# Two linear-attention branches on one core: key-value products by column tiles, a ring of numerator tiles, the Z sums by halves

## The chip, the core and the metric

One of the eight cores of a Trainium2 chip runs the whole program. The metric is the device time of one execution in microseconds; the time given for a kernel is the median of its runs. The core has five engines that run side by side, each through its own list of instructions in order, tied together by semaphores: TensorE (PE in the profile, with its weight loads as PEld), VectorE (DVE), ScalarE (ACT), GpSimd (POOL) and SyncE (SP), which issues DMA transfers. A matmul has a stationary operand (loaded by LDWEIGHTS) and a moving one, and writes to PSUM, which holds eight banks of 512 f32 per partition.

## The reference, cut to what matters

```python
# x: 2048 tokens x 640; 32 heads of 20
def A(x):                                   # branch A
    q, k, v = heads(x @ wqkv)
    phi_q = [softmax(q @ w_phi), softmax(-(q @ w_phi))]      # 40 features a head
    phi_k = the same of k
    kv  = einsum('bhsf,bhsd->bhfd', phi_k, v)
    z   = sum over tokens of phi_k
    num = einsum('bhqf,bhfd->bhqd', phi_q, kv)
    den = einsum('bhqf,bhf->bhq', phi_q, z) + 1e-6
    return (num / den) @ wo
def B(x):                                   # branch B: four segments of 512 tokens
    # causal softmax inside a segment, mixed by sigmoid(beta) with a
    # memory M, z that sums elu features of the earlier segments
    ...
out = g * A(x) + (1 - g) * B(x)             # g = sigmoid(x . gate_w)
```

## The kernel before, in words

The order on all five engines is written out by hand: each engine executes its instructions in the order in which the code emits them. The stages are these.

**Keys and values of branch A** (L300 to L324). After the weights are folded and turned, a loop over 16 chunks of 128 tokens computes keys and values (L235), the two signs of exponentials of the keys (L239, ACT), their sums per head (L243, DVE) and the normalised features `EkSn` (L247, POOL). Each chunk of `EkSn` is also moved by DMA into `Z`, 32 rows of 640 per partition, so that the token sum becomes 31 additions of whole rows (L261, DVE). Then the query weights are folded (L326).

**Key-value products** (L404 to L419). The 640 features are five blocks `j` of 128. For a block and a sign, `emit_kv` (L358) adds 16 matmuls, one a chunk: the stationary operand is 128 features of 128 tokens, the moving one the values of the heads that these features touch (7 heads, 140 columns; 8 heads in two pieces of 80 for block 2). That is 192 matmuls. Only the features of the same head are wanted of each product; `emit_kvn` (L380, DVE) multiplies by a mask and writes `kvn`. The last two chunks of blocks 0, 1, 3, 4 come after the first 14 of all four. On DVE the additions of Z stand among the `emit_kvn`: nine before, four between, 18 after.

**Queries of branch A** (L515 to L527). For two halves of the tokens and five blocks, `emit_pq` computes ten matmuls of 512 columns and ACT takes the exponentials of both signs (L401). All PSUM tiles up to here are of one pool of four tiles of two banks. After the fifth block TensorE turns the finished Z row (`emit_z`, L266). After the sixth, DVE sums 32 sub-rows of it (L274, 31 dependent additions of 20 columns) and writes the denominator weights `kvd` (L277). After the ninth, `emit_den` computes the denominators of chunks 0 to 3, and after the tenth DVE and POOL turn them into scales (`first_chain`, L494).

**The chunk loop of branch A** (L583 to L629). For each of 16 chunks and both signs: TensorE computes the numerators (`emit_num`, L438, six matmuls into one of two PSUM tiles), DVE multiplies them by the scales (`emit_tt`, L487), POOL adds the two signs (L604), and a DMA transposes the sum. TensorE fills its time with 36 halves of projections of branch B (`emit_half`, L546: five matmuls of 320 columns; keys and queries of five chunks, values of eight), whose results ACT copies out. A denominator tile in a bank of its own receives the denominators of the next four chunks (L597); the halves use three more banks. ACT also makes features of keys here (L625 to L627, L618).

**Branch B** (L635 on). 16 steps of two head groups for scores (L679), their exponentials (L683, ACT), triangle masks (L690, POOL), products with values (L735), divisions (`emit_epi`, L755, DVE and POOL), and the remaining projections as filling, by a written plan. Its PSUM pools are, in order, `bst` (two tiles of two banks, scores), `bnd` (`nda`, two banks) and `bps` (two banks). The last part finishes four chunks of rows and writes them out.

Of the kernel before, what the change touches and what calls it, by code (L numbers as in the profile page):

```python
# [15 lines left out]
def kernel(  # L16
# [212 lines left out]
    def emit_a1(sc):  # L229
# [17 lines left out]
        nc.gpsimd.tensor_tensor(  # L247
# [11 lines left out]
    def emit_zadd(ts):  # L259
        for t in ts:  # L260
            nc.vector.tensor_tensor(out=Z[:, 0, :], in0=Z[:, 0, :], in1=Z[:, t, :], op=ALU.add)  # L261
# [7 lines left out]
    def emit_zz(zt_ps):  # L269
        nc.vector.tensor_copy(out=zt, in_=zt_ps)  # L270
        ztv = zt.rearrange("p j (s a h b) -> p j s h b a", s=2, h=2, b=2)
        nc.vector.tensor_copy(out=zz, in_=ztv[:, :, :, :, 0, 0])
        for w in range(1, 32):
            nc.vector.tensor_tensor(out=zz, in0=zz, in1=ztv[:, :, :, :, w // 16, w % 16], op=ALU.add)  # L274
        nc.vector.tensor_tensor(out=zcol, in0=zz[:, :, :, 0], in1=zz[:, :, :, 1], op=ALU.add)
        for sgn in range(2):
            nc.vector.tensor_tensor(out=kvd[:, sgn, :, :, 0], in0=wmask,  # L277
                                    in1=zcol[:, :, sgn:sgn + 1].to_broadcast([P, KC, H]), op=ALU.mult)
# [79 lines left out]
    def emit_kv(j, sgn, scs):  # L358
        h0, h1 = (P * j) // DH, (P * j + P - 1) // DH + 1
        bk, off = int(j > 2), 0  # L360
        n = (h1 - h0) * DH
        b0 = h0 // 16
        if (sgn, j) not in kv_tiles:
            kv_tiles[sgn, j] = w2tile("kv_ps")
            if j < 2:
                kv_tiles[sgn, j + 3] = kv_tiles[sgn, j]
        for sc in scs:
            if h1 <= 16 or h0 >= 16:
                o = 321 * b0 + (h0 - 16 * b0) * DH
                parts = [(off, vA[:, sc].rearrange("p b n -> p (b n)")[:, o:o + n])]  # L370
            else:
                n0 = (16 - h0) * DH
                parts = [(off, vA[:, sc, 0, h0 * DH:320]),
                         (off + n0, vA[:, sc, 1, 0:n - n0])]
            for o, rhs in parts:
                nc.tensor.matmul(kv_tiles[sgn, j][:, bk, o:o + rhs.shape[-1]],
                                 lhsT=EkSn[:, sc, sgn, j * P:(j + 1) * P], rhs=rhs,
                                 start=(sc == 0 and o == off), stop=(sc == NCH - 1 and o == parts[-1][0]))

    def emit_kvn(j, sgn):  # L380
        h0, h1 = (P * j) // DH, (P * j + P - 1) // DH + 1
        g0 = TH[j][0]
        nc.vector.tensor_tensor(
            out=kvn[:, sgn, j, h0 - g0:h1 - g0, :],
            in0=kv_tiles[sgn, j][:, int(j > 2), 0:(h1 - h0) * DH].rearrange("p (h d) -> p h d", d=DH),
            in1=wmw[:, j, h0 - g0:h1 - g0, None].to_broadcast([P, h1 - h0, DH]), op=ALU.mult)
# [4 lines left out]
    def emit_pq(qb, j):  # L391
        Eq = Eq0[:, j] if qb == 0 else a3e.tile([P, 2, HB], BF16, name="Eq")
        pq = w2tile("pq")
        for half in range(2):
            for c in range(KC):
                nc.tensor.matmul(pq[:, half, :], lhsT=WqA[:, c, j * P:(j + 1) * P],  # L396
                                 rhs=xq[:, 2 * qb + half, c],
                                 start=(c == 0), stop=(c == KC - 1))
        pqf = pq.rearrange("p b n -> p (b n)")
# [4 lines left out]
    emit_zadd(range(1, 10))  # L404
    PAIRS = [(js, sgn) for js in ((0, 3), (1, 4)) for sgn in range(2)]
    for js, sgn in PAIRS:
        for j in js:
            emit_kv(j, sgn, range(14))
    for js, sgn in PAIRS:
        for j in js:  # L410
            emit_kv(j, sgn, range(14, NCH))
        for j in js:
            emit_kvn(j, sgn)
    emit_zadd(range(10, 14))
    for sgn in range(2):
        emit_kv(2, sgn, range(NCH))
        emit_kvn(2, sgn)
    emit_gate()
    emit_zadd(range(14, 32))  # L419
# [14 lines left out]

    BATCH = [list(range(c, c + 4)) for c in range(0, NCH, 4)]
    NB = 4

    def emit_num(ch, sgn):  # L438
        qb, qc = divmod(ch, HB // P)
        t = nps.tile([P, 2, 512], F32, name=f"num{sgn}")  # L440
        for n, (j, bk, lo, hi) in enumerate(PIECES):
# [4 lines left out]
                             start=(n in FIRST), stop=(n in LAST))  # L446
        return t[:, :, 0:320].rearrange("p b (h e) -> p b h e", e=DH)

    def emit_den(t, ch, k):
        qb, qc = divmod(ch, HB // P)  # L450
        for sgn in range(2):
            for j in range(KC):
                nc.tensor.matmul(t[:, k, sgn].rearrange("p h e -> p (h e)"),
# [4 lines left out]
    def den_tile():  # L458
        return dps.tile([P, NB, 2, H, 2], F32, name="den")

    def emit_rr(t, n, o=0):
        rr = a3w.tile([P, NB, 2, H], F32, name="rr")
        nc.vector.reciprocal(out=rr[:, 0:n], in_=t[:, o:o + n, :, :, 1])
        return rr, emit_uu(t, rr, n, o)

    def emit_uu(t, rr, n, o):
        uu = a3w.tile([P, NB, 2, H], F32, name="uu", bufs=1)
        nc.vector.tensor_tensor(out=uu[:, 0:n], in0=t[:, o:o + n, :, :, 0], in1=rr[:, 0:n], op=ALU.mult)
        return uu

    def emit_dsum(uu, n):
# [3 lines left out]
        return dd  # L475

# [17 lines left out]
    def first_chain(dt):  # L494
        rr, uu = emit_rr(dt, NB)
# [19 lines left out]
    for qb in range(2):  # L515
        for j in range(KC):
            emit_pq(qb, j)
            if (qb, j) == (0, KC - 1):
                z_den = w2tile("z_den")
                zt_ps = emit_z(z_den[:, 0])  # L520
            if (qb, j) == (1, 0):
                emit_zz(zt_ps)
                open_stages()
            if (qb, j) == (1, 3):
                dt = z_den[:, 1].rearrange("p (k s h e) -> p k s h e", k=NB, s=2, e=2)
                for n in range(NB):
                    emit_den(dt, n, n)  # L527
    emit_gS()
    first_chain(dt)
    aps_stack.close()  # L530
    nps_stack = ExitStack()
    nps, dps, last_pps, pps = [nps_stack.enter_context(tc.tile_pool(
        name=n, bufs=b, space=bass.MemoryType.PSUM, reuse_waits="tile"))
        for n, b in (("nps", 1), ("dps", 1), ("last_pps", 1), ("pps", 2))]
    oTA = resB.tile([P, NCH + 1, KC, P], BF16, name="oTA")
    Msb = resB.tile([P, G, 4, DH + 1], F32, name="Msb")
    Mbd = resB.tile([P, G, 4, DH + 1], BF16, name="Mbd")

    def emit_half_mm(ps, part, sc, half):
        W = {"k": WkB, "q": WqB, "v": WvB}[part]  # L540
        for cc in range(KC):
            nc.tensor.matmul(ps, lhsT=xq[:, sc // 4, cc, sc % 4 * P:(sc % 4 + 1) * P],  # L542
                             rhs=W[:, cc, half * 320:(half + 1) * 320],
                             start=(cc == 0), stop=(cc == KC - 1))

# [18 lines left out]
    for vB in vBs:  # L564
        nc.gpsimd.memset(vB[:, :, :, DH:DH + 1], 1.0)
# [3 lines left out]
              for half in range(2)]  # L569

    def emit_next_half():
        if halves:
            emit_half(last_pps if len(halves) % 3 == 1 else pps, *halves.pop(0),
# [6 lines left out]
    nums = [emit_num(0, 0)]  # L580
    emit_next_half()
    nums.append(emit_num(0, 1))
    for ch in range(NCH):  # L583
# [4 lines left out]
        for sgn in range(2):  # L588
            emit_tt(tt, sgn, nums[sgn], cs_of[ch])
            emit_next_half()  # L590
            if (ch, sgn) in ((4, 1), (9, 1), (14, 1)):
                emit_next_half()
            if ahead and k < 2 and sgn == 0:
                if k == 0:
                    dt = den_tile()
                for n in range(2):
                    emit_den(dt, ahead[2 * k + n], 2 * k + n)  # L597
            if ch + 1 < NCH:
                nums[sgn] = emit_num(ch + 1, sgn)
            if ahead and k == 2 and sgn == 0:  # L600
                uu = emit_uu(dt, rr_n, NB, 0)
# [4 lines left out]
        if ahead and k < 2:  # L606
            if k == 0:
                rr_n = a3w.tile([P, NB, 2, H], F32, name="rr")
            nc.vector.reciprocal(out=rr_n[:, 2 * k:2 * k + 2], in_=dt[:, 2 * k:2 * k + 2, :, :, 1])
# [6 lines left out]
        if ch >= NCH - 2:  # L616
            part = "kq"[ch - NCH + 2]
# [3 lines left out]
        if k == 1:  # L621
            key = stages["k"][(ch // 4) % 2][:, :, 0:DH]
            phik = phiks[0][:, ch // 4, :, 0:DH]
            ek = a3w.tile([P, H, DH], BF16, name="ek")
            nc.scalar.activation(out=ek, in_=key, func=ACT.Relu, scale=-1.0)  # L625
            nc.scalar.activation(out=ek, in_=ek, func=ACT.Exp, scale=-1.0)
            nc.scalar.activation(out=phik, in_=key, func=ACT.Relu)  # L627
        if k == 3:
            nc.gpsimd.tensor_tensor(out=phik, in0=phik, in1=ek, op=ALU.add)  # L629
# [5 lines left out]
    with ExitStack() as bctx:  # L635
# [5 lines left out]
        bst = bctx.enter_context(tc.tile_pool(name="bst", bufs=2, space=bass.MemoryType.PSUM,  # L641
# [3 lines left out]
        bps = bctx.enter_context(tc.tile_pool(name="bps", bufs=2, space=bass.MemoryType.PSUM,  # L645
                                              reuse_waits="tile"))
        oBs, ogs = {}, {}

# [9 lines left out]
        class Step:  # L658
            def __init__(self, k):
                self.s, self.g = divmod(k, G)  # L660
                self.PT = {}
                self.last = k == NSEG * G - 1
                if self.g == 0:
# [63 lines left out]
        def pv_items(st, js):  # L727
            vB = vBs[st.s % 2]

            def piece(j, i):  # L730
                if j == 0 and i == 0 and not st.last:
                    st.nda = bnd.tile([P, 2, 512], F32, name="nda")
# [276 lines left out]
        first_nda = bnd.tile([P, 2, 512], F32, name="nda")  # L1009
        for half in range(2):  # L1010
            banks[1, half] = first_nda[:, half, 0:320]
# [21 lines left out]
        for n, half in ((0, 0), (0, 1), (1, 0), (1, 1)):  # L1033
            turned_mm(n, half, (4,))
# [47 lines left out]
```

## Time and profile before

| | us |
|---|---|
| median of 3 runs (lowest, highest) | 323.62 (323.53, 323.63) |
| the profiled execution, its own time | 324.17 |
| its span, first to last instruction | 322.4 |
| keys, values, folding | 0 to 56.4 |
| key-value products | 56.4 to 66.9 |
| queries, Z, first denominators | 66.9 to 89.9 |
| chunk loop of branch A | 89.9 to 131.8 |
| branch B | 131.8 to 309.5 |
| last rows | 309.5 to 322.4 |

The stages are read off the timeline by the first matmul of each. TensorE is busy for 309.2 us of the span, ScalarE for 252.1, VectorE for 224.7, GpSimd for 208.5. The granted TensorE clock is full in all 40 slices. Busy times of TensorE are modelled: a matmul of 512 columns is shown with 0.38 us, while two such follow each other by 0.216 us, so rates are read from the starts of long rows of matmuls and not from the mean duration.

### The profile page before, as it was taken

How to read it: one execution, taken by the hardware profiler on the slowest of the kernel's cores; microseconds unless marked ns; L12 is line 12 of the kernel's file. 1: busy time of each engine (PE TensorE's matmuls, PEld its weight loads, DVE VectorE, ACT ScalarE, POOL GpSimd, SP SyncE). 2: the span in 40 equal slices, each digit the busy share in tenths (PEclk: the TensorE clock that was granted, in tenths of full speed). 3: DMA queues.
4: the chain of work that ended last, by engine and by line, in shares of the span. 5: the costliest groups of instructions: out<-in, count | busy, mean ns of one | idle time of the engine just before them, and what ended most of it. 6: DMA issues, size and time to landing. Idle time of an engine off the chain costs nothing.

```text
span 322.4 us, 9493 instructions
## 1 busy us (share of the span) xinstructions
PE 309.2 (96%) x3901; PEld 213.5 (66%) x3904; DVE 224.7 (70%) x447; ACT 252.1 (78%) x322; POOL 208.5 (65%) x308
## 2 busy tenths in 40 slices
PE   8999999999999999989999999999999999999995
PEld 7888877964577788555566566656656656655663
DVE  3477997998799797477768577676866745454463
ACT  4777888248945545999998999999998998898953
POOL 8588599302268789756657667677776676666550
PEclk9999999999999999999999999999999999999999
DMA  7948835691016797876231363462476372322132
GB/s 223 218 105 195 204 105 139 190 368 61 0 35 111 113 148 94 160 100 84 52 67 35 66 107 68 87 101 54 79 109 93 72 121 60 76 76 50 47 87 81
DMA packets 91812, 34.19 MB, mean 106 GB/s; under 512 B 79866, under 2 KB 91770, under 8 KB 91770
## 3 DMA queue, kind: packets, MB, share of 16 engines
q1 hardware_dynamic: 91194, 32.95, 50.5%
q10 hardware_dynamic: 576, 0.66, 0.7%
q8 instruction: 30, 0.49, 0.7%
q14 instruction: 12, 0.10, 0.1%
HBM read 6.42 MB, written 2.62 MB: 28 GB/s over the span
## 4 chain that ended last, share of the span: by engine, by line
PE 37%; ACT 22%; DVE 3%; issue 2%; POOL 0%; ACTq 0%; DVEq 0%
ACT PT L683 19%; PE st_ps L679 9%; PE proj L813 7%; PE nda L735 6%; PE proj L869 5%; PE proj L542 3%; PE num L443 2%; DVE td L772 1%; PE nda L748 1%; PE nda L743 1%; DVE rec L762 1%; ACT ek L841 1%; PE nda L991 1%; DVE rec L760 1%; DVE Eq L845 1%
## 5 line engine op out<-in xcount | busy, mean ns | idle before, releaser
L683 ACT ACTIVATE PT<-st_ps 128x1024 bf16<-128x1024 f32 x160 | 153.8, 1024 | 14.7 <-PE st_ps L679 12.5
L690 POOL TENSOR_SCALAR_AFFINE_SELECT PT<-PT 128x512 bf16<-128x512 bf16 (+1 forms) x130 | 85.4, 675 | 48.5 <-ACT PT L683 48.3
L735 PEld LDWEIGHTS <-PT 128*128 128x128 bf16 x1280 | 39.8, 96 | 10.3 <-issue 6.5
L247 POOL TENSOR_TENSOR EkSn<-Ek,krec 128x1280 bf16<-128x1280 bf16 x16 | 37.4, 2360 | 9.1 <-DVE krec L246 8.3
L735 PE MATMUL nda<-vB,PT 128*128 128x21 bf16 x1240 | 41.4, 173 | 0.7 <-DVE mtmp L778 0.6
L869 PEld LDWEIGHTS <-xTf 128*128 128x128 bf16 x300 | 26.5, 97 | 16.0 <-issue 7.1
L875 DVE CAST Z<-proj 128x320 bf16<-128x320 f32 x44 | 20.8, 487 | 22.2 <-PE proj L869 21.8
L235 PEld LDWEIGHTS <-xTf 128*128 128x128 bf16 x240 | 27.1, 113 | 5.9 <-DVE xTf L200 0.3
L243 DVE TENSOR_REDUCE ksum<-Ek 128x64 f32<-128x1280 bf16 x16 | 23.6, 1475 | 8.0 <-ACT Ek L239 8.0
L489 DVE TENSOR_TENSOR tt<-num,rr 128x640 f32<-128x640 f32 x32 | 24.8, 802 | 4.9 <-POOL rr L482 2.2
L239 ACT ACTIVATE Ek<-pk 128x640 bf16<-128x640 f32 x32 | 20.8, 702 | 9.4 <-PE pk L235 8.4
L679 PE MATMUL st_ps<-Z 32*128 32x512 bf16 (+3 forms) x256 | 24.7, 299 | 3.5 <-ACT PT L683 2.9
L604 POOL TENSOR_TENSOR oA<-tt 128x640 bf16<-128x640 f32 x16 | 24.6, 1548 | 4.6 <-DVE tt L489 3.4
L813 PE MATMUL proj<-WkA,oTA 128*128 128x320 bf16 x160 | 27.1, 299 | 0.3 <-DMA oTA<-oA 0.3
L679 PE MATMUL st_ps<-Eq 32*128 32x512 bf16 (+3 forms) x256 | 24.5, 299 | 2.3 <-ACT PT L683 1.8
L775 POOL TENSOR_TENSOR oB<-td 128x320 bf16<-128x320 f32 x22 | 19.5, 886 | 6.5 <-DVE td L772 4.9
L401 ACT ACTIVATE Eq<-pq 128x1024 bf16<-128x1024 f32 x20 | 19.4, 1021 | 5.4 <-PE pq L396 5.4
L813 PE MATMUL proj<-WvA,oT 128*128 128x320 bf16 x120 | 22.2, 300 | 0.5 <-DVE oTA L822 0.5
L396 PE MATMUL pq<-xTf,WqA 128*128 128x512 bf16 x97 | 21.9, 379 | 0.2
L772 DVE TENSOR_TENSOR td<-nda,rec 128x640 f32<-128x640 f32 x23 | 19.0, 825 | 2.1
L542 PEld LDWEIGHTS <-xTf 128*128 128x128 bf16 x180 | 16.3, 97 | 4.4
L443 PE MATMUL num<-kvn,Eq 128*128 128x240 bf16 (+2 forms) x192 | 18.0, 229 | 0.6 <-DVE tt L489 0.6
(174 smaller groups left out, 552.8 us busy)
## 6 DMA issues: line engine op xcount, KB each, us to landing
Z<-EkSn SPq DMA_DIRECT2D x32, 160.0 KB, 2.7
out_dram<-orow SPq DMA_DIRECT2D x8, 160.0 KB, 1.8
out_dram<-oTA SPq DMA_DIRECT2D x6, 160.0 KB, 1.9
WvA<-in_A_wqkv_dram SPq DMA_DIRECT2D x2, 400.0 KB, 6.3
WkB<-in_B_wk_dram SPq DMA_DIRECT2D x1, 800.0 KB
WqB<-in_B_wq_dram SPq DMA_DIRECT2D x1, 800.0 KB, 6.9
WvB<-in_B_wv_dram SPq DMA_DIRECT2D x1, 800.0 KB, 9.6
WkA<-in_A_wo_dram SPq DMA_DIRECT2D x1, 800.0 KB, 11.3
```

Of the source, the lines that this page charges most:

```text
L235: nc.tensor.matmul(ps[:, bk, 0:n], lhsT=key_tokens(c, sc), rhs=rhs, start=(c == 0), stop=(c == KC - 1))
L247: nc.gpsimd.tensor_tensor(out=EkSn[:, sc].rearrange("p s (h f) -> p (s h) f", f=DH), in0=Ek.rearrange("p s (h f) -> p (s h) f", f=DH), in1 ...
L443: nc.tensor.matmul(t[:, bk, (lo - 16 * bk) * DH:(hi - 16 * bk) * DH], lhsT=Eqs[qb, j][:, sgn, qc * P:(qc + 1) * P], rhs=kvn[:, sgn, j, lo ...
L489: nc.vector.tensor_tensor(out=tt[:, sgn].rearrange("p (b h) d -> p b h d", b=2), in0=ps, in1=csb, op=ALU.mult)
L542: nc.tensor.matmul(ps, lhsT=xq[:, sc // 4, cc, sc % 4 * P:(sc % 4 + 1) * P], rhs=W[:, cc, half * 320:(half + 1) * 320], start=(cc == 0), s ...
L604: nc.gpsimd.tensor_tensor(out=oA.rearrange("p (h d) -> p h d", d=DH), in0=tt[:, 0], in1=tt[:, 1], op=ALU.add)
L679: nc.tensor.matmul(ps[:, i - i0, o:o + L - c * P], lhsT=kT[32 * i:32 * i + 32, c * P:(c + 1) * P], rhs=qT[32 * i:32 * i + 32, c * P:L], st ...
L683: nc.scalar.activation(out=PT[:, i0:i0 + 2], in_=ps, func=ACT.Exp, scale=SCALE_B)
L690: nc.gpsimd.affine_select(out=v, in_=v, pattern=[[0, n_i], [1, P]], compare_op=ALU.is_ge, fill=0.0, base=0, channel_multiplier=-1)
L735: nc.tensor.matmul(nd[:, j, i], lhsT=block(st, c)[:, i, (j - c) * P:(j - c + 1) * P], rhs=vB[:, c, 4 * st.g + i, :], start=(c == 0), stop= ...
L813: nc.tensor.matmul(ps, lhsT=oT[:, k % KC], rhs=W[:, k % KC, hs], start=(k == 0), stop=(k == n - 1))
L869: nc.tensor.matmul(ps, lhsT=xq[:, sc // 4, k, sc % 4 * P:(sc % 4 + 1) * P], rhs=W[:, k, half * 320:(half + 1) * 320], start=(k == 0), stop ...
```

## The change

Key-value products: for every chunk but the first, the 128 features of a block are split into four groups of 32. Each group is a matmul of its own, with 32 stationary columns at column position 0, 32, 64 or 96 of the array, and only the two or three heads that its features touch as moving columns (40 or 60). The four write to different 32 partitions of one PSUM tile. The first chunk stays one matmul of 128 features (it also starts the accumulation). Both signs of a block share a tile, so that one `emit_kvn` serves both. In the order, blocks 0 to 3 take chunks 1 to 13, then 14 and 15, and block 4 follows in the tile of block 0.

The 16th chunk of `EkSn` is made by VectorE. Each addition of Z is two, of 320 columns each, six before the `emit_kvn` of blocks 0 to 3, two before that of block 4, 23 after; the 31 additions of sub-rows are two each as well, and the two products of `kvd` are one.

The values of chunks 0 and 4 are computed among the queries (the order is five query blocks, values 0, Z, four query blocks, denominators, values 4, the tenth block), which leaves 32 halves for the chunk loop. The numerators there are a ring of three PSUM tiles, three ahead; the denominators of two chunks at a time go into the unused columns 320 to 447 of a numerator tile, and VectorE reads them just behind its multiplication. The halves use two banks. The features of keys are spread over other chunks.

In branch B the PSUM pools stand in the order `bps`, `bnd`, `bst`, and `nda` is one tile for all steps. At the end the first four rows are copied out before the last five matmuls, which go into the first score tile.

```diff
-        nc.gpsimd.tensor_tensor(
+        (nc.vector if sc == NCH - 1 else nc.gpsimd).tensor_tensor(
             out=EkSn[:, sc].rearrange("p s (h f) -> p (s h) f", f=DH),
...
-            nc.vector.tensor_tensor(out=Z[:, 0, :], in0=Z[:, 0, :], in1=Z[:, t, :], op=ALU.add)
+            for lo in (0, D // 2):
+                cols = slice(lo, lo + D // 2)
+                nc.vector.tensor_tensor(out=Z[:, 0, cols], in0=Z[:, 0, cols], in1=Z[:, t, cols], op=ALU.add)
...
-            nc.vector.tensor_tensor(out=zz, in0=zz, in1=ztv[:, :, :, :, w // 16, w % 16], op=ALU.add)
+            for js in (slice(0, 3), slice(3, KC)):
+                nc.vector.tensor_tensor(out=zz[:, js], in0=ztv[:, js, :, :, 0, 0] if w == 1 else zz[:, js],
+                                        in1=ztv[:, js, :, :, w // 16, w % 16], op=ALU.add)
...
+        f0, f1 = (P * j, P * j + P) if group is None else (P * j + 32 * group, P * j + 32 * group + 32)
+        h0, h1 = f0 // DH, (f1 - 1) // DH + 1
...
+        at = {} if group is None else {"tile_position": (0, 32 * group)}
...
+                nc.tensor.matmul(kv_tiles[j][f0 - P * j:f1 - P * j, sgn, (lo - base) * DH:(hi - base) * DH],
+                                 lhsT=EkSn[:, sc, sgn, f0:f1],
+                                 rhs=vA[:, sc, b, (lo - 16 * b) * DH:(hi - 16 * b) * DH],
+                                 start=(sc == 0 and n == 0), stop=(sc == NCH - 1 and n == len(parts) - 1), **at)
...
+    def emit_kv_groups(j, scs):
+        for sc in scs:
+            for sgn in range(2):
+                for group in range(4):
+                    emit_kv(j, sgn, [sc], group)
...
+    emit_zadd(range(1, 7))
+    for j in range(4):
+        for first in ([0], [1, 2, 3], [], [])[j]:
+            for sgn in range(2):
+                emit_kv(first, sgn, [0])
+        emit_kv_groups(j, range(1, 14))
+    for j in range(4):
+        emit_kv_groups(j, range(14, NCH))
+        emit_kvn(j)
+    emit_zadd(range(7, 9))
+    for sgn in range(2):
+        emit_kv(4, sgn, [0])
+    emit_kv_groups(4, range(1, NCH))
+    emit_kvn(4)
     emit_gate()
-    emit_zadd(range(14, 32))
+    emit_gS()
+    emit_zadd(range(9, 32))
...
+    EARLY_V = [0, 4]
...
+    for what in "pppppvzppppdvp":
...
-    nps, dps, last_pps, pps = [nps_stack.enter_context(tc.tile_pool(
+    nps, pps = [nps_stack.enter_context(tc.tile_pool(
         name=n, bufs=b, space=bass.MemoryType.PSUM, reuse_waits="tile"))
-        for n, b in (("nps", 1), ("dps", 1), ("last_pps", 1), ("pps", 2))]
+        for n, b in (("nps", 3), ("pps", 2))]
...
+            emit_num_at(2 * ch + sgn + 3)
...
-        bst = bctx.enter_context(tc.tile_pool(name="bst", bufs=2, space=bass.MemoryType.PSUM,
+        bps = bctx.enter_context(tc.tile_pool(name="bps", bufs=2, space=bass.MemoryType.PSUM,
...
-        bps = bctx.enter_context(tc.tile_pool(name="bps", bufs=2, space=bass.MemoryType.PSUM,
+        bst = bctx.enter_context(tc.tile_pool(name="bst", bufs=2, space=bass.MemoryType.PSUM,
...
+        nda = bnd.tile([P, 2, 512], F32, name="nda")
...
-        banks[2, 1] = bnd.tile([P, 2, 512], F32, name="nda")[:, 0, 0:320]
-        fill(2, 1, range(KC))
...
+        for n, half in both[0]:
+            evict(n, half)
+        banks[2, 1] = pair_ps[0][:, 0, 0:320]
+        fill(2, 1, range(KC))
```

The denominators of the last part of the chunk loop, and what the lines of the changed kernel are (L247 `EkSn`, L263 additions of Z, L373 key-value products, L387 `kvn`, L400 queries, L451 numerators, L499 their products with the scales, L529 and L581 the halves and their copies, L719 scores), follow from the same diff.

## The prediction

> **What bounds the kernel now.** I read the page's busy row, then the busy time by stage, then the timeline around each stage's first matmul.
>
> ```profile
> PE 309.2 (96%) x3901; PEld 213.5 (66%) x3904; DVE 224.7 (70%) x447; ACT 252.1 (78%) x322; POOL 208.5 (65%) x308
> ```
> ```profile
> 56.40:66.90 10.50, 10.50 (x201) 10.39 (x199) 10.16 (x22) 1.78 (x3) 2.81 (x2) 1.00 0.77 235
> 66.90:89.90 23.00, 22.84 (x149) 11.27 (x149) 19.22 (x63) 17.63 (x19) 4.16 (x6) 1.00 0.33 111
> 89.90:131.80 41.90, 41.30 (x494) 33.61 (x491) 35.49 (x51) 24.32 (x51) 34.28 (x36) 1.00 0.69 109
> 131.80:309.50 177.70, 170.17 (x2476) 105.99 (x2476) 113.68 (x254) 162.96 (x178) 120.11 (x204) 1.00 0.45 79
> ```
>
> The columns are stretch, length, then PE, PEld, DVE, ACT, POOL busy. From 56 to 132 us PE has no gap worth naming: moving work between these stages saves nothing, only work taken off PE does. DVE is nearly full in the first (10.16 of 10.50), so it bounds next. In branch B ACT and PE take turns; a later start there moves the end one for one.
>
> ```profile
> 47.59 11.62 POOL L247 TENSOR_TENSOR EkSn<-Ek,krec 128x1280 bf16<-128x1280 bf16 x5
> ...
> 56.45 10.44 PE L376 MATMUL kv_ps<-vA,EkSn 128*128 128x140 bf16 x192
> ...
> 56.90 6.87 DVE L261 TENSOR_TENSOR Z<-Z 128x640 bf16<-128x640 bf16 x9
> ...
> 63.77 1.78 DVE L383 TENSOR_TENSOR kvn<-kv_ps,wmw 128x140 bf16<-128x140 f32 x8
> ...
> 67.90 9.43 DVE L261 TENSOR_TENSOR Z<-Z 128x640 bf16<-128x640 bf16 x18
> ...
> 79.06 6.59 DVE L274 TENSOR_TENSOR zz<-zz,zt 128x20 bf16<-128x20 bf16 x31
> ```
>
> Here one sees the Z chain run beside PE: 31 additions, then (77.5 to 77.95) the turn on PE, 31 small additions, `kvd` ready at 86.47, and PE's denominators at 86.63. PE only just did not wait.
>
> **Key-value products.** Before: 192 matmuls, 10.5 us from 56.45 to the queries at 66.93. After: 12 whole matmuls (0.5 us at this mean of 0.054), about six changes between array shapes (estimated 0.1 us each, the idle beside L679 below), and 150 quads of four tiles. No row here shows column tiles. The bounds come from two rows:
>
> ```profile
> 131.81 0.10 PEld L679 LDWEIGHTS <-Z 32*128 32x128 bf16 x4 [0.26 <-issue]
> 131.82 0.40 PE L679 MATMUL st_ps<-Z 32*128 32x512 bf16 x4
> 131.92 0.49 DVE L553 CAST vB<-proj 128x320 bf16<-128x320 f32 x1 [0.53 <-PE proj L542]
> ...
> 141.71 0.56 PE L735 MATMUL nda<-vB,PT 128*128 128x21 bf16 x16
> ```
>
> Small matmuls with their loads follow each other by (0.56-0.17)/15 = 0.026 us: a quad whose tiles overlap wholly costs that, one whose tiles take turns 0.104. Four row tiles of 512 columns take 0.40 us together, where one is 0.38 and four in turn would be 1.03: they overlap, with 0.007 for each further tile. Nearest to this, 0.026 to 0.046; I take 0.035. So PE ends blocks 0 to 3 at 56.45+0.9+120*0.035 = 61.5.
>
> The Trainium skill (TensorE: Matmul & The Clock Gate, Part 3) reports 2.38 times for three column tiles; by that efficiency a quad would be an estimated 0.033.
>
> **VectorE's chain decides instead.** `EkSn` of chunk 16 waits for POOL's 15th (59.21-2.36 = 56.85) and costs what the sum of 1280 elements costs (L243, 1.48): 58.35. `xg` 0.3. Its two DMAs into Z leave SP 0.9 earlier than from POOL's 59.21, and so do the five weight loads queued behind them on SP; the early values need WvB, which landed 9.6 after its issue at 61.74, in time for 74.4. The first addition of Z in the trace lasted 2.66 instead of 0.49, up to the end of POOL's `EkSn`; that cover is gone. The two fills of `vB` (1.24) now stand on POOL beside the additions: bounds 0 and 1.24, taken as 0, since the small additions at 79.06 to 82.4 kept their 0.18 beside POOL's fills (L511, L513). A whole addition of Z is 0.526 from start to start ((9.43-0.49)/17); it waits for its predecessor. Halves wait for the one before last, which is done. A half by the rows of 20 (0.18) and 640 columns (0.49) lasts 0.33; independent instructions overlap by 0.08 (eight `kvn` of 0.293 in 1.78), so 0.25. Bounds: 0.16 (the columns alone) and 0.36 (no overlap); 0.25 is the row-based middle. Twelve halves: 61.65. `kvn` of both signs 0.38 to 0.43 each, the first done at 62.1, the fourth at 63.3. Block 4 needs the tile of block 0: PE waits 61.5 to 62.1, then 30 quads, gate, and the queries start at 63.6 instead of 66.93. PE gains 3.3 here.
>
> **Queries.** PE: 63.6, five blocks at 2.16, one value chunk 1.36 (ten at 0.136): 75.8. DVE: four halves 1.0, `kvn` 0.4, `emit_gS` 0.65, 46 halves 11.5: 76.8. So PE waits 1.0 for Z. The turn 0.3, four blocks 8.64, denominators 1.17, values 1.36, tenth block 2.16: the numerators start at 90.4 (before 89.95), with two value chunks already done. `kvd` is ready by 77.1+0.17+0.52+31*0.21+0.75 = 85.1, before the denominators at 85.7: cover 0.6; gone, PE waits for the rest. The small halves save next to nothing, as each still waits about 0.21 for itself. ACT has 1.94 per 2.16 and two copies of 0.7 more: hidden.
>
> **Chunk loop.** PE: numerators 0.40, half 0.68, two chunks' denominators 0.58 (starts in the timeline). 32*1.08+6*0.58 = 38.0 against 41.9. DVE: about 9.2 per four chunks with a wait of 0.5 for POOL's scales, under PE's 9.8, and the ring of three covers the jitter; 0.3 left as stall. It ends at 128.7.
>
> **Handover to branch B: a new wait.** In the order of the changed program the last value half is still copied by DVE (L581), but its copy now stands ahead of the two products (L499) of chunk 15, and the first scores on PE wait for the VectorE signal that the second of these gives. Before, the products were done at 131.39 and the copy (131.92) held up nobody. Now: copy 0.2 after PE's last half and 0.42 long, products 0.74 and 0.82: PE idles 2.2 us. Behind the waiting scores on PE stand the first projections of branch B, for which DVE's copies wait, and ACT has no exponential (L683) to take. Bounds: 0, if the rest catches up, and 2.2; ACT is busy 163 of 178 us in branch B, so I take all of it. First scores at 130.9 instead of 131.82. The gain of 3.1 has shrunk to 0.9.
>
> **The rest.** The wait of 0.34 at 137.3 for the transposed last chunk goes, since two such DMAs no longer queue: -0.3. One `nda` tile: its first matmul still waits for L778's product: 0. The last five matmuls can follow PE's 318.2 instead of 318.37: -0.15. Pools moved in PSUM: 0, bounds -0.3 to 0.3.
>
> **Sum:** -0.9-0.3-0.15 = -1.35, on 324.17: 322.8. The profiled execution lies 0.55 over the median, so 322.3 in runs.
>
> **Rivals.**
> - **The tiles take turns** (the slower side). PE reaches the queries at 58+150*q; up to q = 0.044 VectorE hides it, at 0.053 it is even, and at 0.104 the numerators start at 99.4 and branch B 8.1 later: 331.3. For it: 0.026 holds for all short matmuls here, whatever their width. Against: the row tiles. Chance 0.17. The Trainium skill (the same part, The mechanism) lets a weight load pass running matmuls only if their row groups differ; column tiles share all rows, so by that rule this is what happens. The row-tile burst can't tell, since its row groups do differ.
> - **Instructions arrive too slowly.** Packets of instructions (below): 7805/30 = 260 each, 0.7% of 16 engines or 1.2 us each; one at a time gives 37 ns per quad of eight instructions, hidden; half as much again, 0.055, gives 324.0. Chance 0.13.
>
> ```profile
> q8 instruction: 30, 0.49, 0.7%
> ```
>
> - **Half additions cost more than 0.25.** There are 62 ahead of the turn. At 0.30 Z is 62*0.05 = 3.1 later and PE waits for it: 325.4. At 0.16 PE is the bound and gets back its waits of 0.6 and 1.0: 320.7. Chance of the first 0.10.
> - **The change's new wait is covered**, if PE's or ACT's work lets B catch up: 320.2. Against: ACT's share there. Chance 0.08.
>
> **From this to the numbers.** Forecast 0.52 (0.48 of it faster, 0.04 within). Within means 0.2%, 0.65 us, about what a measurement of this kernel tells from no change. Instructions: 0.08 same, 0.05 slower; halves: 0.04 same, 0.06 slower; the covered wait faster; turns slower. Faster 0.56, same 0.16, slower 0.28. The range 320.0 to 326.0 takes in halves at 0.16 and 0.30, the covered wait, and quads up to 0.068, and leaves out the tiles in turn (0.17).
>
> **What would show it.** Four starts of L373 in some 0.035; queries at 63.6; PE idle before the turn of Z (L268) by about 1.0, ended by DVE L263; first numerators at 90.4; PE idle of 2.2 us before the first L719, ended by DVE L499. Wrong: L373 taking over 8 us; stalls by DVE L499 inside the chunk loop; no idle at the handover.

## The result and the profile after

The changed kernel takes 336.55 us (median of 6 runs, 335.09 to 337.94) against 323.62 (6 runs): a ratio of 1.0392, 95% interval 1.0373 to 1.0411, slower by some 13 us where 322.3 had been forecast. Its profiled execution took 336.53, with a span of 334.8. No engine is busy for longer than before by more than 0.2 us, but TensorE has 4324 matmuls where it had 3901. The page's busy row and its row of instruction packets:

```profile
PE 309.4 (92%) x4324; PEld 212.3 (63%) x4324; DVE 224.3 (67%) x506; ACT 252.3 (75%) x320; POOL 207.3 (62%) x307
...
q8 instruction: 34, 0.56, 0.7%
```

TensorE's busy time has grown by 0.2 us, the span by 12.4: the loss is idle time of TensorE. The busy time by stage tells where (cut at the changed kernel's own marks: first key-value product, first query, first numerators, first scores, end; columns as before: length, PE, PEld, DVE, ACT, POOL, then the granted clock, the share of the 16 DMA engines, GB/s):

```profile
56.40:76.60 20.20, 8.61 (x623) 7.30 (x621) 7.41 (x24) 1.81 (x4) 0.52 (x1) 0.72 0.78 250
76.60:103.40 26.80, 26.80 (x171) 13.43 (x168) 23.41 (x120) 18.91 (x21) 5.57 (x9) 0.96 0.01 2
103.40:143.76 40.36, 38.27 (x473) 31.71 (x472) 34.85 (x52) 23.85 (x47) 34.41 (x34) 1.00 0.71 118
143.76:334.80 191.04, 180.97 (x2616) 114.45 (x2616) 118.88 (x268) 166.33 (x185) 121.47 (x207) 0.99 0.42 78
```

The key-value stage has doubled, from 10.5 to 20.2 us, with TensorE busy for only 8.6 of them. The other stages are near what was forecast: queries to numerators 26.8, the chunk loop 38.3 and 2.1 of idle time behind it. TensorE's timeline in the key-value stage (start, length, line, operands, count; in brackets the idle time ahead and what ended it):

```profile
58.26 0.69 PE L373 MATMUL kv_ps<-vA,EkSn 128*128 128x140 bf16 x43 [0.18 <-ACT WqA L190]
60.03 1.22 PE L373 MATMUL kv_ps<-vA,EkSn 128*32 128x40 bf16 x128 [1.08 <-issue]
65.14 1.59 PE L373 MATMUL kv_ps<-vA,EkSn 128*32 128x40 bf16 x128 [3.88 <-issue]
71.61 2.25 PE L373 MATMUL kv_ps<-vA,EkSn 128*32 128x60 bf16 x128 [4.88 <-issue]
75.33 1.09 PE L373 MATMUL kv_ps<-vA,EkSn 128*32 128x40 bf16 x73 [1.48 <-issue]
```

Two things are to be read here. The bursts are of 128 matmuls each time, whichever block of features they belong to; with their weight loads that is 256 instructions. And what ends the idle time is "issue", time in which the profile shows nothing that TensorE waits for: no engine, no data, and no semaphore instruction of TensorE's own stands in this stage. It is 11.3 us in all. The trace also records when each packet of instructions of that queue was moved (0.56 MB in 34, so 16.4 KB each, or 64 bytes for each of 256 instructions):

```
us                  1st           2nd           3rd           4th
packet moved        57.66-58.53   62.61-63.68   69.18-70.29   72.96-74.06
next burst begins   60.03         65.14         71.61         75.33
```

Each burst begins 1.3 to 1.5 us behind the end of a packet. So TensorE does the 128 short matmuls in some 1.2 us (1.6 and more at a halved clock) and then has no instructions until the next packet is there. A second loss follows from the idle time, in the granted clock (the third column from the right):

```profile
60.00:64.00 4.00, 1.22 (x128) 1.11 (x128) 1.23 (x6) 0.00 (x0) 0.00 (x0) 1.00 0.93 272
64.00:68.00 4.00, 1.59 (x128) 1.44 (x128) 0.00 (x0) 0.00 (x0) 0.00 (x0) 0.65 1.07 373
68.00:72.00 4.00, 0.40 (x40) 0.40 (x42) 0.00 (x0) 0.00 (x0) 0.00 (x0) 0.50 1.07 362
```

The clock is halved from about 65 until 78.9 us, so that the first queries, too, run at half speed until then: 50 of their matmuls take 11.9 us where before they took 10.8. The column beside it shows the DMA engines full: the five weight loads of 0.8 MB each, issued from 59.7 on, are moved just then.

### The profile page after: what moved, and what is told of

Its sections match the earlier page's. It is cut to its first block, busy times and chain, and to the rows that moved or that the text cites. A ratio compares the mean times of both kernels' runs of the same rounds, so it can differ in the third digit from the quotient of the medians.

```text
span 334.8 us, 10366 instructions
## 1 busy us (share of the span) xinstructions
PE 309.4 (92%) x4324; PEld 212.3 (63%) x4324; DVE 224.3 (67%) x506; ACT 252.3 (75%) x320; POOL 207.3 (62%) x307
## 4 chain that ended last, share of the span: by engine, by line
PE 65%; ACT 20%; issue 6%; DVE 4%; POOL 3%; ACTq 0%; DVEq 0%; POOLq 0%
ACT PT L723 18%; PE st_ps L719 8%; PE proj L851 7%; PE pq L400 7%; PE pk L235 7%; PE proj L529 6%; PE pv L235 6%; PE nda L773 6%; PE proj L907 5%; PE num L451 4%; PE kv_ps L373 2%; POOL oB L813 1%; PE num L468 1%; DVE Eq L883 1%; ACT WqA L190 1%
## 5 line engine op out<-in xcount | busy, mean ns | idle before, releaser
L773 PEld LDWEIGHTS <-PT 128*128 128x128 bf16 x1280 | 40.5, 96 | 8.8 <-issue 5.2
L247 POOL TENSOR_TENSOR EkSn<-Ek,krec 128x1280 bf16<-128x1280 bf16 x15 | 35.1, 2361 | 9.2 <-DVE krec L246 8.5
L907 PEld LDWEIGHTS <-xTf 128*128 128x128 bf16 x300 | 26.9, 99 | 16.6 <-issue 7.1
L235 PEld LDWEIGHTS <-xTf 128*128 128x128 bf16 x240 | 27.1, 113 | 5.9 <-DVE xTf L200 0.3
L719 PE MATMUL st_ps<-Z 32*128 32x512 bf16 (+3 forms) x256 | 25.0, 305 | 5.9 <-ACT PT L723 3.7
L499 DVE TENSOR_TENSOR tt<-num,rr 128x640 f32<-128x640 f32 x32 | 25.0, 812 | 4.5 <-POOL rr L492 1.7
L719 PE MATMUL st_ps<-Eq 32*128 32x512 bf16 (+3 forms) x256 | 25.0, 299 | 2.0 <-ACT PT L723 1.6
L400 PE MATMUL pq<-xTf,WqA 128*128 128x512 bf16 x100 | 23.2, 392 | 0.0
L907 PE MATMUL proj<-WkB,xTf 128*128 128x320 bf16 x110 | 19.5, 314 | 0.0
L719 PEld LDWEIGHTS <-Z 32*128 32x128 bf16 x256 | 7.5, 92 | 18.7 <-issue 17.5
```

What stands on the lines that cost most here:

```text
L235: nc.tensor.matmul(ps[:, bk, 0:n], lhsT=key_tokens(c, sc), rhs=rhs, start=(c == 0), stop=(c == KC - 1))
L247: (nc.vector if sc == NCH - 1 else nc.gpsimd).tensor_tensor(out=EkSn[:, sc].rearrange("p s (h f) -> p (s h) f", f=DH), in0=Ek.rearrange("p ...
L499: nc.vector.tensor_tensor(out=tt[:, sgn].rearrange("p (b h) d -> p b h d", b=2), in0=ps, in1=csb, op=ALU.mult)
L719: nc.tensor.matmul(ps[:, i - i0, o:o + L - c * P], lhsT=kT[32 * i:32 * i + 32, c * P:(c + 1) * P], rhs=qT[32 * i:32 * i + 32, c * P:L], st ...
L773: nc.tensor.matmul(nd[:, j, i], lhsT=block(st, c)[:, i, (j - c) * P:(j - c + 1) * P], rhs=vB[:, c, 4 * st.g + i, :], start=(c == 0), stop= ...
L907: nc.tensor.matmul(ps, lhsT=xq[:, sc // 4, k, sc % 4 * P:(sc % 4 + 1) * P], rhs=W[:, k, half * 320:(half + 1) * 320], start=(k == 0), stop ...
```

## The experiments

**Theory**: TensorE runs out of instructions; a packet's round trip (asked for, moved, usable) sets the pace, and the weight loads make that round trip longer. **Rivals**: the loads alone are the cause; the column tiles are slow in themselves; another part of the change holds TensorE back. A second theory concerns the handover to branch B: the copy ahead of the last products costs 2.1 us of idle time and some clock.

### The weight loads held back (e1)

```diff
+    nc.sync.dma_start(out=zt[0:1, 0, 0:4], in_=kvn[0:1, 0, 4, 0, 0:4])
     for W, src in ((WkB, B_wk), (WqB, B_wq), (WvB, B_wv)):
         nc.sync.dma_start(out=W, ...)
```

> The changed kernel, but the five 0.8 MB weight loads on SP wait until the last key-value block has been scaled (L387), by a four-element copy ahead of them. In the changed kernel PE takes the short matmuls of L373 in bursts of 128 with 'issue' waits of 1.1, 3.9, 4.9 and 1.5 us between them, one burst behind each 16 KB instruction packet. Supply theory: PE runs out of instructions; the round trip of a packet is about 3.7 us without other transfers (from the last one, after the loads) and 5.1 to 6.5 beside the loads. Then the waits shrink but stay: bursts at about 60.0, 63.7, 67.4 and 71.1, queries (L400) near 72.5 instead of 76.97, time about 332. Rival A, the loads alone are the cause: no waits over 0.5 us in L373, queries at 64 to 66, time 323 to 325. Rival B, the short tiles themselves are slow or take turns: nothing moves, 336 to 337.

332.32 us (331.80 to 333.11), ratio 1.0263 [1.0244, 1.0282]. The timeline of TensorE:

```profile
60.01 1.36 PE L373 MATMUL kv_ps<-vA,EkSn 128*32 128x40 bf16 x128 [1.14 <-issue]
64.28 1.41 PE L373 MATMUL kv_ps<-vA,EkSn 128*32 128x40 bf16 x128 [2.92 <-issue]
68.01 2.25 PE L373 MATMUL kv_ps<-vA,EkSn 128*32 128x60 bf16 x128 [2.32 <-issue]
71.74 1.09 PE L373 MATMUL kv_ps<-vA,EkSn 128*32 128x40 bf16 x73 [1.48 <-issue]
```
```profile
64.00:68.00 4.00, 1.41 (x128) 1.25 (x128) 0.00 (x0) 0.00 (x0) 0.00 (x0) 0.61 0.02 4
```

The same bursts of 128, now 3.7 to 4.3 us apart instead of 3.7 to 6.5; queries at 73.0. The packets begin 1.0 to 1.2 us behind the start of a burst, take 1.1 to 1.7, and are used 1.3 to 1.5 later: the round trip is some 3.6 us on idle DMA engines (their share between 64 and 72 us is 0.02, the last column but one). Beside the loads, in the changed kernel, the second and third packet take no longer to be moved (1.07 and 1.11), but begin only 2.6 and 4.0 us behind the start of a burst; what they wait for there is not shown. The loads thus cost 4 us of the loss, and not the rest: they alone are not the cause.

### Whole matmuls, all else as changed (e2)

```diff
         for sc in scs:
             for sgn in range(2):
-                for group in range(4):
-                    emit_kv(j, sgn, [sc], group)
+                emit_kv(j, sgn, [sc])
```

> The changed kernel with the key-value products as whole 128-feature matmuls again (192 in place of 612), everything else as in the change. Supply theory: L373 runs without a wait in about 10.6 us, queries at about 67.1, Z's chain then sets the turn at about 80.1, numerators at 93.7, chunk loop 38.1, handover idle 2.1, first scores near 133.9; time about 326.7, so the column tiles carry 10 of the 13 us lost and the rest of the change loses some 3. Rival, another part (Z by halves, EkSn of chunk 16 on VectorE, the early values) holds PE back: time stays above 333.

326.11 us (325.32 to 326.50), ratio 1.0063 [1.0044, 1.0082]. Three lines of its chain of work (start, length, what) carry it:

```profile
56.49 10.40 PE kv_ps L373 x192
67.36 1.07 DVE eg L354
68.92 2.91 DVE Z L263 x13
```

The products run through in 10.4 us without a wait, and the queries begin at 66.91. The column tiles carry 10.4 of the 13 us; the rest of the change loses 2.2. Behind the products VectorE is late for Z: it takes up the gate (L354 to L356) before the remaining additions.

### Column tiles spread between the queries (e3)

The five blocks of key-value products are taken one by one, each followed by a block of queries; the loads are held as in e1.

```diff
+    for j in range(KC):
+        for sgn in range(2):
+            emit_kv(j, sgn, [0])
+        emit_kv_groups(j, range(1, NCH))
+        emit_kvn(j)
+        ...
+        emit_zadd(next(zadds))
+        emit_pq(0, j)
...
-    for what in "pppppvzppppdvp":
+    for what in "zppppdvvp":
```

> Column tiles kept, with the same 612 matmuls, but block by block with one block of queries (10 long matmuls, 2.16 us) behind each, so that 128 short matmuls are asked for every 3.6 us instead of every 1.1; the weight loads wait as in the run with late loads, and both early value chunks stand behind the denominators. Supply theory: no 'issue' wait over 1 us among L373, the fifth query block ends near 76 (before: 77.5; changed kernel: 88.6), Z's chain sets the turn near 76.5, numerators near 91.5, first scores near 131.7; time about 324. Rival B, the short tiles are slow in themselves (5 us per 128): fifth query block near 90, time 335 or more.

334.98 us (334.42 to 336.12), ratio 1.0347 [1.0322, 1.0373]: the expected time was missed by 11 us, and this run decides nothing on its own. The timeline shows why:

```profile
60.50 1.35 PE L373 MATMUL kv_ps<-vA,EkSn 128*128 128x140 bf16 x122
...
63.95 1.45 PE L373 MATMUL kv_ps<-vA,EkSn 128*128 128x80 bf16 x124
66.14 2.32 PE L400 MATMUL pq<-xTf,WqA 128*128 128x512 bf16 x10 [0.74 <-ACT Eq L407]
70.49 1.35 PE L373 MATMUL kv_ps<-vA,EkSn 128*128 128x140 bf16 x122 [2.03 <-ACT Eq L407]
```

The blocks of products run through, 122 matmuls in 1.35 us, with no wait for issue. But from the third block of queries on TensorE waits again and again for ScalarE's exponentials (0.74, then 2.03, 2.03 and 1.75 us): the four PSUM tiles of the pool are handed out in another order than by turns, and a new block gets the tile whose reader has just begun. The first numerators wait in the same way for the last exponentials (2.03). The theory of the supply is not touched, but a wait that the new order brought in hid it.

### Fixed PSUM tiles (e5), and the loads not held (e6)

```diff
+    ring = [w2tile("ring") for _ in range(4)]
-            kv_tiles[j] = w2tile("kv_ps")
+            kv_tiles[j] = ring[j % 2]
-        pq = w2tile("pq")
+        pq = ring[2 + j % 2] if qb == 0 else w2tile("pq")
...
-    for what in "zppppdvvp":
+    for what in "vzppppdvp":
```

In both the last half is copied by ScalarE and the gate's three operations stand behind Z's chain. In e5 WvB is loaded at once and the other four weights wait for the last block of products; in e6 none waits.

> Column tiles spread between the query blocks as in the run before with spread tiles, but with fixed PSUM tiles in turn (two for key-value blocks, two for query blocks), so that a block of queries no longer waits for ScalarE's exponentials of the block just ahead of it. WvB is loaded at once and the other four weights wait for the last key-value block. Also: the last value half is copied by ScalarE, and the gate's three VectorE operations stand behind Z's chain. Supply theory: 128 short matmuls per 3.6 us are within what packets bring (3.7 us each at worst); fifth query block ends near 76.3, numerators near 91.3, first scores near 130.3 after 0.9 idle, time 321.5 to 322.5, faster than the kernel before (323.9). Rival, some other cost of column tiles (a change of array shape dearer than 0.15 us, or waits for VectorE's scaling): fifth query block after 79, time 325 or more.

> The same as the run with WvB first, but no weight load is held back: all five follow Z's copies at 59.7, as in the changed kernel. Supply theory with contention: beside the loads (60 to 74 us) a packet takes 5.1 to 6.5 us and 138 matmuls are asked for every 3.6, so PE still runs dry two or three times for 1 to 2.5 us, fifth query block near 80, time about 326. Rival, the loads do not delay packets once PE is not idle (the packet is asked for earlier): the same as with the held loads, 322.

e5: 322.64 us (320.52 to 324.83), ratio 0.9965 [0.9941, 0.9989]. e6: 326.37 (326.03 to 327.02), ratio 1.0078 [1.0066, 1.0091]. In e5 the numerators begin at 91.2 and the first scores at 130.4, as expected; the two waits for issue that are left among the key-value products and the queries are 0.65 and 0.55 long. Two of its blocks of products, one with a wait ahead and one without:

```profile
64.43 1.03 PE L374 MATMUL ring<-vA,EkSn 128*32 128x60 bf16 x105 [0.65 <-issue]
...
67.56 1.64 PE L374 MATMUL ring<-vA,EkSn 128*128 128x140 bf16 x122
```

In e6:

```profile
65.18 1.03 PE L374 MATMUL ring<-vA,EkSn 128*32 128x60 bf16 x105 [0.62 <-issue]
...
71.65 1.35 PE L374 MATMUL ring<-vA,EkSn 128*32 128x40 bf16 x109 [2.86 <-issue]
```

The same 612 matmuls that took 20 us are hidden among the queries once they are asked for at the pace of the packets; column tiles are not slow. With the loads beside them packets come 5.1 and 6.4 us apart in e6 (starts at 57.64, 62.76, 69.19), and TensorE stands again, for 0.62 and 2.86 us, with 3.4 us at half the clock behind the longer wait.

### Half as many instructions (e8, e9)

The tiles are made 64 features wide (two of 64 instead of four of 32; 312 matmuls), in e8 in the place and order of the change, in e9 in the kernel of e5.

```diff
-... (P * j + 32 * group, P * j + 32 * group + 32)
+... (P * j + 64 * group, P * j + 64 * group + 64)
-        at = ... {"tile_position": (0, 32 * group)}
+        at = ... {"tile_position": (0, 64 * group)}
-                for group in range(4):
+                for group in range(2):
```

> The changed kernel with column tiles of 64 features instead of 32, in the same place and order: 312 matmuls in place of 612, the loads not held back. It asks whether the count of instructions or the column tiles as such bring the waits. Supply theory: some 157 matmuls are there at the start and each packet brings 128, so the second packet (near 60.0) carries PE to the 285th and the last 27 wait for one more packet beside the loads (near 65); queries near 65.7, Z's turn near 78.5, first scores near 132.5, time about 325. Rival, column tiles stall as such: waits in L373 as often as in the changed kernel, time 330 or more.

> The run with spread 32-feature tiles and held loads, with 64-feature tiles instead (312 matmuls). There PE still stood still three times before the turn (0.8, 0.3 and 0.9 us). Supply theory: with half the instructions these waits go, the pairs cost about as much as the quads (0.038 against 0.033), so the time falls by 0 to 2 us, to 321 to 322.6, and the runs spread less than the 320.5 to 324.8 there. Rival, the waits there were not for instructions: no change in the waits, 322.6 or more.

e8: 323.75 us (322.99 to 325.41), ratio 1.0001 [0.9985, 1.0017], 13 us under the changed kernel by the width of the tiles alone:

```profile
56.23 6.72 PE L373 MATMUL kv_ps<-vA,EkSn 128*128 128x140 bf16 x283
64.40 0.74 PE L373 MATMUL kv_ps<-vA,EkSn 128*64 128x80 bf16 x29 [1.45 <-issue]
...
77.94 0.58 PE L268 MATMUL z_den<-ident_b,Z 128*128 128x128 bf16 x5 [0.34 <-DVE Z L263]
```

After 283 matmuls, two less than expected, the last 29 wait once for a packet. So the count of instructions brings the waits, not column tiles as such. e9 is the fastest version: 321.27 us (321.05 to 321.41), ratio 0.9919 [0.9905, 0.9934] to the kernel before. It has no wait for issue in these stages; a pair of tiles costs 0.037 us (0.038 had been expected), a quad in e5 0.032.

### The handover, and the smallest repair (e4, e7, e10)

e4 is the changed kernel with the first of these two edits alone, the copy of the last half. e7 adds both, the copy and the gate behind Z's chain, to e2; e10 adds both to e8.

```diff
-                      nc.scalar.copy if halves else nc.vector.tensor_copy)
+                      nc.scalar.copy)
...
-    emit_gS()
     emit_zadd(range(9, 32))
...
+    emit_gS()
     first_chain(dt)
```

> The changed kernel with the last value half copied by ScalarE instead of VectorE, so that nothing stands ahead of the last two products (L499) on VectorE. Handover theory: PE's idle time before the first scores (L719) falls from 2.1 us to about 0.9, and if the granted clock then stays at 1.00 (it falls to 0.50 for 3.2 us behind the idle time in the changed kernel) the gain is larger than the idle time: 334 to 335 instead of 336.55. Rival, branch B catches up: 336.5, unchanged.

> The run with whole 128-feature matmuls, and in addition the last value half copied by ScalarE and the gate's three VectorE operations behind Z's chain. Theory of the rest: in the run with whole matmuls alone Z's chain set the turn at 80.1, 0.9 behind PE, and the handover cost 2.1 of idle and 1.05 of halved clock; now PE sets the turn at 79.3, numerators at 92.7, first scores at 131.7 after 0.9 idle; time 322.9 to 323.6, at or just under the kernel before. Rival, the handover's idle time is made up for in branch B and the Z chain does not move: 326.

> The run with 64-feature tiles in the place of the change, and in addition the last value half copied by ScalarE and the gate's three VectorE operations behind Z's chain: the smallest edit of the changed kernel that the findings suggest. There PE waited 0.64 for Z and 2.1 before the first scores. Theory: Z no longer waits (-0.6), the handover idle falls to 0.9 (-1.2) and the clock stays up (-0.5 to -1.0 where it fell): 321.0 to 321.7. Rival, the packet's wait in the key-value products grows by as much, or branch B catches up: 323 or more.

e4: 335.19 us (334.69 to 336.32), ratio 1.0354 [1.0333, 1.0376]. The handover in the changed kernel, from its timeline, then one of its stretches:

```profile
141.71 0.49 DVE L581 CAST vB<-proj 128x320 bf16<-128x320 f32 x1 [0.71 <-PE proj L529]
...
142.11 1.55 DVE L499 TENSOR_TENSOR tt<-num,rr 128x640 f32<-128x640 f32 x2
...
143.76 0.61 PE L719 MATMUL st_ps<-Z 32*128 32x512 bf16 x4 [2.09 <-issue]
```
```profile
145.00:146.00 1.00, 1.00 (x6) 0.57 (x4) 0.09 (x1) 1.00 (x2) 0.33 (x1) 0.50 0.47 94
```

and in e4:

```profile
143.51 0.40 PE L719 MATMUL st_ps<-Z 32*128 32x512 bf16 x4 [0.90 <-DVE tt L499]
```
```profile
145.00:146.00 1.00, 0.63 (x10) 0.18 (x8) 0.28 (x1) 1.00 (x2) 1.00 (x1) 1.00 0.75 147
```

In the changed kernel the two products start only behind the copy, at 142.11, and TensorE idles for 2.09 us; the clock is then halved from 143.7 to 147.1. (The idle time is put down to "issue" here, since a semaphore instruction of TensorE's weight loads, not the matmul, does the waiting: it lasts 3.2 us, from 140.5 to 143.7. The products end at 143.66, which gives the releaser.) With the copy on ScalarE the idle time is 0.90 and the clock stays at 1.00. From the first scores to the end e4 takes 190.0 us and the changed kernel 191.1, so branch B does not catch up: the idle time costs 1.2 and the clock 1.0. The medians differ by 1.4 and not by 2.2. In the profiled executions the rest is made up of a key-value stage that is 0.6 longer in e4, where the clock also stays halved until 80.1.

e7: 323.41 us (322.74 to 323.90), ratio 0.9983 [0.9974, 0.9991], as expected: without column tiles and with the two repairs, the rest of the change is worth some 0.5 us. e10: 322.41 us (321.10 to 324.85), ratio 0.9964 [0.9939, 0.9988], 0.7 above the expected bound. Its profiled execution took 321.45, with queries at 64.4 and first scores at 129.3; four of its twelve runs lie above 323.8, and these four are the ones with a mean clock under 0.996. It fits that a packet came late in them and the clock fell, but none of them was profiled: open.

## Why the prediction was wrong

- **The step that failed** is the term of the key-value products, queries at 63.6, which let the supply of instructions cost nothing. That rested on the price given under the rival "Instructions arrive too slowly": "7805/30 = 260 each, 0.7% of 16 engines or 1.2 us each; one at a time gives 37 ns per quad of eight instructions, hidden; half as much again, 0.055, gives 324.0." The mechanism was named, with a chance of 0.13, and its price was wrong by a factor of 3 to 6. The 1.2 us is the time in which a packet is moved (0.9 to 1.7 measured). From packet to packet it is 3.5 to 4.3 us on idle DMA engines (e1) and up to 6.6 beside the weight loads in the changed kernel, that is 0.11 to 0.21 per quad of tiles. In this stage of the kernel before, packets came 11.1 and 10.7 us apart (57.5, 68.6, 79.3), and nowhere in its trace closer than 6.8 (259.2 to 266.0). TensorE was not seen to ask for more, so the trace showed that a packet can come every 6.8 us, 0.21 per quad, and nothing of a faster pace. That was the upper bound to be used, and the change asked for a packet every 1.0 us. The queries began at 76.6 instead of 63.6: 13.0 of the 13.7 us by which the profiled execution missed its forecast.
- **The DMA engines.** The prediction noted that the weight loads would leave SP 0.9 us earlier, and asked only whether WvB would be there in time. Whether the loads would hold up the packets of instructions was not asked; holding the loads back took 4 us off (e1).
- **The tiles themselves** were right: forecast 0.035 a quad; in a burst at full clock the starts are 0.0080 apart, 0.032 a quad. The Trainium skill (TensorE: Matmul & The Clock Gate, Part 3, The mechanism) has a weight load overlap running matmuls only where their row groups differ; the trace does not agree, as these tiles share all rows and still start 0.0080 apart with their loads. The efficiency in the table of that part, by which 0.033 was estimated, does agree. That "the tiles take turns" gave 331.3, the value nearest to the result, is chance.
- **The crossing from packet to packet** showed in no wait of TensorE for "issue" in this stage of the kernel before, and for 11.3 us here. The Trainium skill (Runtime: NRT & Kernel Launch, Instruction fetch mechanics) states blocks of 16 KiB of 256 instructions, which the packets of 16.4 KB and the bursts of 128 pairs bear out. It also states that the crossing from block to block is mostly hidden, which holds in the kernel before and not here.
- **Z's chain**: a half addition 0.235 from start to start (forecast 0.25), right. The forecast wait of TensorE for Z, 1.0, did not show, as TensorE was 13 us late itself; where the products are quicker it does (0.34 in e8 and in e2). In the kernel before, the turn of Z begins at 77.72 and not at 77.5 as the prediction reads it; nothing hangs on this. `kvd` is ready at 98.02 and the denominators begin at 98.75: cover 0.7, forecast 0.6.
- **Queries to numerators** 26.8, forecast 26.8; of the measured time 1.1 is the halved clock, in place of the wait of 1.0. **The chunk loop** 38.3, forecast 38.0 and a stall of 0.3; there is no stall by L499.
- **The handover**: idle 2.09, forecast 2.2 and by the products (L499) as said. Right in place and size, but a second loss was missed: the clock falls behind it, for another 1.0.
- **Branch B and the tail**: forecast -0.45. Where the clock stays up it is -0.6 (e4: 190.0 against 190.6); in the changed kernel the clock turns it into +0.4.

The sum: 322.8 forecast for the profiled execution, +13.0 until the numerators, -0.1 until the first scores, +0.9 behind them, which gives 336.6; 336.5 was measured.

## What to carry to other kernels

A trace shows the supply of instructions only at the pace at which the kernel took them. Where a change makes instructions shorter and more, count them in blocks of 256, ask how many microseconds each block lasts, and compare that with the round trip of a packet (3.6 us here, more beside large loads), not with the time in which it is moved. If the pace is too fast, halve the count (wider tiles) or put long matmuls between the short ones, and keep large loads out of that stage: all three, with the two repairs behind them, made a loss of 3.9% into a gain of 0.8%. Price an idle time of TensorE of two microseconds together with the slow clock that may follow it.

## What the runs showed of the hardware

- Packets of 256 instructions follow each other by 3.5 to 4.3 us on idle DMA engines where TensorE is ready for each (e1), and by 5.0 and 6.6 beside loads that move 360 GB/s (the changed kernel).
- Column tiles of 32 features begin 8.0 ns apart, and a pair of 64 features takes 37 ns; small whole matmuls with their loads had been 26 ns apart.
- An idle time of 2.1 us before the first scores was followed by 3.4 us at half the clock (the changed kernel, e2 and e8); one of 0.9 was not (e4). The length of the idle time alone does not decide: in e3 one of 2.03 us, up to 70.5, was followed by no slow clock, and the next of the same length, up to 76.1, by a slow clock from 77.3 to 80.7.
- Apart from the start and the end of the execution, the stretches at half the clock lasted 3.4 us or a multiple of it: 10.2 in e1, 13.7 in the changed kernel (65.2 to 78.9, 2.3 us behind the first query), 17.1 in e4.
